# Output products by Strassen's algorithm, with all later steps in a new list

## The chip, the cores and the metric

The kernel runs on one core of one Trainium2 chip. The metric is the device time of one execution in microseconds. The core's engines are TensorE (PE in the profile; its weight loads are PEld), VectorE (DVE), ScalarE (ACT), GpSimd (POOL) and SyncE (SP), which here only issues DMAs. TensorE writes only into PSUM, which the kernel uses as four buffers of two banks (128 x 1024 fp32 each). GpSimd does no work out of PSUM in this kernel.

## The reference

```python
def _attn_ref(q, k, v, sort_net):          # batch 4, heads 8, seq 768, head_dim 64, 8 blocks of 96
    P = sort_net                           # (4, 8, 8, 8), five rounds of exp and row/column norms
    ...
    k_sorted = np.einsum('bhij,bhjcd->bhicd', P, k_b)
    v_sorted = np.einsum('bhij,bhjcd->bhicd', P, v_b)
    scores = scale * np.matmul(q_b, k_sb.transpose(0, 1, 2, 4, 3))     # inside a block
    attn = softmax(scores)
    return np.matmul(attn, v_sb)

def _moe_ref(x, w1, w2, w_out):            # x (3072, 512), w1, w2 (512, 1024), w_out (1024, 512)
    g = np.maximum(x @ w1, x @ w2)
    return g @ w_out                       # float32 (3072, 512)
```

## The kernel before

There are four batch items of 768 tokens. For each item the kernel mixes the blocks of k and of v with the Sinkhorn matrix (`sort_k`, `sort_v_pair` and its relatives, matrix products whose results go from PSUM to `kT` and `v_sb`), computes the scores of 8 units (`scores`: 8 small products, then one exponential on ScalarE into one of 8 buffers `e`), multiplies with the values (`values`: 8 products, then a reciprocal and a multiplication on VectorE), and transposes the result to `xT` (`x_transposes`: on TensorE for item 0, by a DMA from the SP queue for the others). The queries of items 2 and 3 are copied into pairs (`pair_q`) and transposed by two DMAs on SP (`q_transposes`). `turn_v` reorders the loaded v on chip, in four pieces for each pair of rows.

The second half uses max(a, b) = relu(a - b) + b. `w_difference` turns w1 into w1 - w2, `moe_h` computes the relu part into tiles `g` (8 tiles an item, each 128 x 2 x 384: two rows of 128 hidden features for half of the tokens, `ch`), and `w_product` computes `wc` = w2 @ w_out once. An item's output is then g @ w_out + x @ wc: a product of 768 tokens by 1536 features by 512 columns. In `out_products` it is done in six tiles of 128 tokens, each of 12 matmuls with a moving operand of 128x512 that accumulate in one bank; `moe_out` evicts two tiles at a time (128x1024) and stores 512 KB, and `moe_out_last` does the last two tiles in smaller pieces.

The order is written out by hand. Up to the step `h11b` of `front` all is item 0's attention, its `g` tiles and the transposed w2. From there a loop over the items runs through units (`moe_h`, `w_product`, `moe_out`), and the lists `first_tail`, `second_tail` and `third_tail` say which attention steps of the next item come after which unit. Each engine works through its instructions in that order; the steps differ in which engine evicts PSUM (`pick` and `evac` choose by running loads). The loads go through GpSimd's DMA queue, the stores and the DMA transposes through SP's.

Of the kernel before, what the change touches and what calls it, by code (L numbers as in the profile page):

```python
# [16 lines left out]
def kernel(  # L17
# [35 lines left out]
    NE = 8  # L53
# [188 lines left out]
    def turn_v(rows, eng, c0, c1):  # L242
        dst, src = v_dc[rows, 0 : D * BLK], v_raw[rows]
        if eng == "A":
            nc.scalar.copy(
                out=dst.rearrange("p (d c two) -> p d c two", c=BLK, two=2)[:, :, c0:c1],
                in_=src.rearrange("p (c d two) -> p d c two", c=BLK, two=2)[:, :, c0:c1],
            )
        else:
            nc.vector.tensor_copy(  # L250
                out=dst.bitcast(U32).rearrange("p (d c) -> p d c", c=BLK)[:, :, c0:c1],
                in_=src.bitcast(U32).rearrange("p (c d) -> p d c", c=BLK)[:, :, c0:c1],
            )
# [149 lines left out]
    def pair_q(b, two):  # L403

        if two == 0:
            q_pair[b] = qpool.tile([128, HP, R, 2 * D], BF16, tag="q_pair", name="q_pair", bufs=1)
        nc.vector.tensor_copy(
            out=q_pair[b][:, :, :, two * D : (two + 1) * D],
            in_=q_raw[b][:, two * HP : (two + 1) * HP].rearrange("p h (r d) -> p h r d", r=R),
        )  # L410
        load["D"] += 900
# [125 lines left out]
    e_tiles, x_tiles = {}, {}  # L537

    def scores(b, u, n=0):
# [15 lines left out]
        e = e_bufs[(b * 8 + u) % NE]  # L555
# [98 lines left out]
    def w_product(dmt):  # L654
# [9 lines left out]
        evac(wc[:, dmt, :], ps[:, 0:512], 512)  # L664
# [33 lines left out]
    out_ps = {}  # L698

    def out_products(dst, b, ti, n0=0, n1=512, part=None):  # L700
        ch, off = divmod(ti * 128, TCH)
        for m in range(NFB + HP) if part is None else range(part * 6, part * 6 + 6):
            hp = m - NFB
            nc.tensor.matmul(  # L704
                dst,
                g_tiles[b, ch, m // 2][:, m % 2, off : off + 128]
                if m < NFB
                else xT[:, b % 2, ch, hp % 2, hp // 2, off : off + 128],
                wo_sb[:, m, n0:n1] if m < NFB else wc[:, hp, n0:n1],
                start=(m == 0),  # L710
                stop=(m == NFB + HP - 1),
            )

    def moe_out(b, ti, part):
        slot = ti % 2
        if slot == 0 and part == 0:
            out_ps[0] = ps_f32("out_ps")
        ps = out_ps[0]
        out_products(ps[:, slot * 512 : (slot + 1) * 512], b, ti, part=part)
        if slot == 1 and part == 1:  # L720
            tok0 = b * S + ti * 128
            o = opool.tile([128, 2, 512], FP32, tag="o", name="o")
            evac(o.rearrange("p t n -> p (t n)"), ps, 1024)
            nc.sync.dma_start(
                out=out[tok0 - 128 : tok0 + 128, :].rearrange("(t p) n -> p t n", p=128),
                in_=o,
            )

    def moe_out_last(ti, pieces):

        tok0 = (B - 1) * S + ti * 128
        for n0, n1, eng in pieces:
            ps = ps_f32("out_ps")
            out_products(ps[:, 0 : n1 - n0], B - 1, ti, n0, n1)
            o = opool.tile([128, n1 - n0], FP32, tag=f"o{ti}{n0}", name="o", bufs=1)
            if eng == "A":
                nc.scalar.copy(out=o, in_=ps[:, 0 : n1 - n0])
            else:
                nc.vector.tensor_copy(out=o, in_=ps[:, 0 : n1 - n0])  # L739
# [107 lines left out]
    def turn(rows, c0):  # L847
        turn_v(rows, "D", c0, c0 + 24)
        load["D"] += 850

    def sorts_and_scores(b):
        SC, VA, TR = att(b)
        return SC, VA, TR, [lambda t=t: sort_k(b, t) for t in range(3)]

    SC, VA, TR, KS = sorts_and_scores(1)
    VS = [lambda t=t: sort_v_pair(2, t) for t in range(8)]
    TQ = [lambda half=half: q_transposes(1, half) for half in range(2)]
    TURN = [lambda c=c: turn(both, c) for c in (0, 24, 48, 72)]
    first_tail = {
        7: KS,  # L860
        9: [TQ[0], TURN[0]],
        10: [SC[0], TQ[1], TURN[1]],
        11: SC[1:4] + TURN[2:4] + [lambda half=half: load_v(3, half=half) for half in range(2)],
        12: VS[0:3],
        13: VS[3:6],
        14: VS[6:8] + [SC[4]],
        15: [VA[0], lambda: pair_q(2, 0)],
        16: [VA[1], lambda: pair_q(2, 1)],
        17: SC[5:8] + [TR[0]],
        18: [VA[2]],  # L870
        19: [VA[3], TR[1]],
        20: [VA[4]],
        21: [VA[5], TR[2]],
        22: [VA[6], VA[7], TR[3]],
    }
    SC, VA, TR, KS = sorts_and_scores(2)
    VS = [lambda t=t: sort_v_halved(3, t) for t in range(4)]
    TURN = [lambda c=c: turn(both, c) for c in (0, 24, 48, 72)]
    second_tail = {
        0: [lambda: q_transposes(2, 0), lambda: q_transposes(2, 1)],  # L880
        2: KS,
        4: SC[0:2],
        5: [VA[0]],
        6: SC[2:4] + [TURN[0]],
        7: [VA[1], TR[0]],
        8: [VA[2], TURN[1]],
        9: [VA[3], TR[1], TURN[2]],
        10: SC[4:7],
        11: [VA[4], TURN[3]],
        12: [VA[5], TR[2], lambda: load_k(3), lambda: load_q(3)],  # L890
        13: [VA[6]],
        14: SC[7:8] + VS[0:2],
        15: [VA[7], TR[3]],
        16: VS[2:4],
        17: [lambda: pair_q(3, 0)],
        18: [lambda: pair_q(3, 1)],
    }
# [70 lines left out]
```

## Time and profile before

| | before |
|---|---|
| device time, median of 3 runs | 165.8 us (165.71 to 165.83) |
| span of the profiled execution, first to last instruction | 165.0 us |
| TensorE busy | 157.0 us (95%) |
| VectorE busy | 77.5 us (47%) |
| ScalarE busy | 82.3 us (50%) |
| GpSimd busy | 33.9 us (21%) |
| mean granted TensorE clock | 0.999 |

The profiled execution has no separate device time beside its span. Its span is 0.8 us below the median of the runs, so 0.8 us lies around the span, and a time for the changed kernel is made as a span plus 0.8 us. In the timeline a matmul's duration runs to its modelled end and overlaps the next one's; a pace is therefore read as the distance between the starts of two groups, divided by the number of matmuls between them. The list that the change replaces begins at 38.40 us, where the first `sort_k` of item 1 follows the last `moe_h` of item 0, and TensorE's last matmul ends at 161.9 us.

### The profile page before, as it was taken

To read this page: it belongs to the slowest core of one execution; us is meant where nothing else is said; L and a number is where in the kernel's file an instruction comes from. 1 tells how busy PE (TensorE), PEld (TensorE's weight loads), DVE (VectorE), ACT (ScalarE), POOL (GpSimd) and SP (SyncE) were. 2 spreads that over 40 slices of the span, in tenths; PEclk is the share of its full clock that TensorE was granted. 3 is DMA by queue.
4 is the path that set the end of the run, shared out by engine and by line. 5 is a ranking of instruction groups with operands and counts; after the bars stand their busy time and mean duration, and the time that the engine had idled before them with its cause. 6 is when DMAs were issued, how large, how long until landed. Compare 5 with 4: busy or idle time off the path is not lost.

```text
span 165.0 us, 4561 instructions
## 1 busy us (share of the span) xinstructions
PE 157.0 (95%) x2007; PEld 95.4 (58%) x2025; DVE 77.5 (47%) x170; ACT 82.3 (50%) x101; POOL 33.9 (21%) x61
## 2 busy tenths in 40 slices
PE   7889999999999999999999999999999999999992
PEld 7839776756554555557655554575655546654451
DVE  4878995684366564525277763250642420000011
ACT  3489776617239846055652353457447206642020
POOL 7949997131206000000014010000000000000000
PEclk9999999999999999999999999999999999999999
DMA  3999999999999999689515999995025294000333
GB/s 41 204 204 194 164 196 207 209 205 220 210 203 204 220 224 167 175 84 228 111 19 104 126 212 157 200 309 29 0 52 175 50 164 142 0 0 0 127 131 127
DMA packets 30404, 23.90 MB, mean 145 GB/s; under 512 B 16752, under 2 KB 25200, under 8 KB 30384
## 3 DMA queue, kind: packets, MB, share of 16 engines
q0 software_dynamic: 11040, 13.37, 50.0%
q1 hardware_dynamic: 19200, 10.17, 28.9%
q8 instruction: 16, 0.26, 0.7%
q10 hardware_dynamic: 144, 0.07, 0.1%
q14 instruction: 4, 0.03, 0.1%
HBM read 26.75 MB, written 6.29 MB: 200 GB/s over the span
## 4 chain that ended last, share of the span: by engine, by line
PE 81%; DMA 6%; DVE 5%; ACT 3%; POOL 2%; issue 2%
PE out_ps L704 37%; PE h_ps L677 25%; DMA w_sb<-in_moe_w_dram 5%; PE wc_ps L657 4%; PE o_ps L575 4%; PE k_ps L458 3%; PE s_ps L548 3%; ACT e L556 1%; POOL w_sb L189 1%; PE v_ps L523 1%; DMA p_sb<-in_sort_net_dram 1%; PE tq_ps L433 1%; DVE colsum L276 1%; DVE p_sb L273 1%; PE tw_ps L638 1%
## 5 line engine op out<-in xcount | busy, mean ns | idle before, releaser
L704 PE MATMUL out_ps<-wo_sb,g 128*128 128x512 bf16 (+2 forms) x187 | 46.0, 370 | 1.4 <-issue 1.0
L677 PE MATMUL h_ps<-xT,w_sb 128*128 128x384 bf16 x256 | 44.5, 326 | 0.0
L677 PEld LDWEIGHTS <-w_sb 128*128 128x128 bf16 x256 | 24.0, 98 | 15.5
L556 ACT ACTIVATE e<-s_ps 96x768 bf16<-96x768 f32 x32 | 24.0, 805 | 14.8 <-PE s_ps L548 14.8
L691 ACT ACTIVATE g<-h_ps 128x768 bf16<-128x768 f32 x27 | 21.7, 811 | 17.4 <-PE h_ps L677 17.3
L704 PEld LDWEIGHTS <-g 128*128 128x128 bf16 x200 | 17.1, 97 | 15.8
L704 PE MATMUL out_ps<-wc,xT 128*128 128x512 bf16 (+2 forms) x98 | 24.7, 370 | 0.1
L108 ACT COPY o<-out_ps 128x1024 f32<-128x1024 f32 x10 | 10.1, 1012 | 28.0 <-PE out_ps L704 25.2
L592 DVE TENSOR_TENSOR x<-o_ps,rs 96x512 bf16<-96x512 f32 x32 | 22.0, 687 | 1.1
L704 PEld LDWEIGHTS <-xT 128*128 128x128 bf16 x100 | 9.6, 97 | 11.2
L575 PEld LDWEIGHTS <-e 96*128 96x128 bf16 x256 | 11.7, 97 | 5.7 <-DVE v_sb L110 0.2
L586 DVE RECIPROCAL rs<-o_ps 96x8 f32<-96x8 f32 x32 | 6.4, 201 | 17.2 <-PE o_ps L575 17.1
L739 DVE COPY o<-out_ps 128x512 f32<-128x512 f32 (+1 forms) x2 | 1.2, 625 | 27.6 <-PE out_ps L704 27.6
L575 PE MATMUL o_ps<-v_sb,e 96*128 96x65 bf16 x256 | 12.7, 193 | 0.0
L110 DVE CAST kT<-k_ps 128x1024 bf16<-128x1024 f32 x6 | 7.2, 1222 | 8.4 <-PE k_ps L458 8.4
L110 DVE CAST v_sb<-v_ps 96x1024 bf16<-96x1024 f32 x7 | 8.5, 1219 | 4.9 <-PE v_ps L523 2.2
L160 POOL DMA_DIRECT2D v_raw<-in_k_dram x3 | 2.5, 838 | 35.1 <-DVE v_dc L250 31.4
L108 ACT CAST v_sb<-v_ps 96x1024 bf16<-96x1024 f32 x9 | 8.8, 1015 | 1.6 <-PE v_ps L500 0.8
L169 POOL DMA_DIRECT2D v_raw<-in_v_dram x11 | 6.5, 593 | 12.7 <-DVE v_dc L250 6.4
L693 DVE TENSOR_SCALAR g<-h_ps 128x768 bf16<-128x768 f32 x5 | 4.8, 957 | 8.9 <-PE h_ps L677 8.8
L548 PEld LDWEIGHTS <-kT 64*128 64x128 bf16 x256 | 6.1, 94 | 4.8 <-issue 2.6
L548 PE MATMUL s_ps<-qT,kT 64*128 64x96 bf16 x256 | 8.5, 204 | 0.3 <-DVE qT L110 0.2
(97 smaller groups left out, 144.4 us busy)
## 6 DMA issues: line engine op xcount, KB each, us to landing
out_dram<-o SPq DMA_DIRECT2D x11, 512.0 KB, 3.4
v_raw<-in_v_dram POOLq DMA_DIRECT2D x8, 384.0 KB, 13.5
k_raw<-in_k_dram POOLq DMA_DIRECT2D x9, 256.0 KB, 11.0
w_sb<-in_moe_w_dram POOLq DMA_DIRECT2D x4, 256.0 KB, 6.0
w_sb<-in_moe_w_dram POOLq DMA_DIRECT2D x2, 512.0 KB, 9.6
wo_sb<-in_moe_w_out_dram POOLq DMA_DIRECT2D x2, 512.0 KB, 13.7
v_raw<-in_v_dram POOLq DMA_DIRECT2D x3, 256.0 KB, 5.0
q_raw<-in_q_dram POOLq DMA_DIRECT2D x4, 192.0 KB, 9.1
```

Source lines behind the costliest of these rows:

```text
L108: nc.scalar.copy(out=out_ap, in_=in_ap)
L110: nc.vector.tensor_copy(out=out_ap, in_=in_ap)
L169: nc.gpsimd.dma_start(out=v_raw[r0 : r0 + 64, m * n : (m + 1) * n], in_=v_src[b, :, m * n : (m + 1) * n],)
L548: nc.tensor.matmul(ps[:, h2 * 512 + ii * 128 : h2 * 512 + ii * 128 + BLK], kT[b][rows, (hp * 8 + i) * BLK : (hp * 8 + i) * BLK + 128], rhs ...
L556: nc.scalar.activation(out=e[:, 0 : 8 * BLK].rearrange("p (t c r) -> p t c r", t=8, r=R), in_=ps[0:BLK] .rearrange("p (t f) -> p t f", t=8 ...
L575: nc.tensor.matmul(ps[:, h2 * 512 + ii * 65 : h2 * 512 + (ii + 1) * 65], e[:, (h2 * 4 + ii) * BLK : (h2 * 4 + ii) * BLK + 128], v_sb[:, m0 ...
L586: nc.vector.reciprocal(out=rs, in_=ov[:, :, :, 64])
L592: nc.vector.tensor_tensor(out=x, in0=ov[:, :, :, 0:D], in1=rs.to_broadcast([BLK, 2, 4, D]), op=ALU.mult,)
L657: nc.tensor.matmul(ps[:, 0:512], w2T[:, fb, dmt * 128 : (dmt + 1) * 128], wo_sb[:, fb, :], start=(fb == 0), stop=(fb == NFB - 1),)
L677: nc.tensor.matmul(h_ps[ch, t][:, m * 512 : m * 512 + TCH], w1_sb[:, hp, fb * 128 : (fb + 1) * 128], xT[:, b % 2, ch, hp % 2, hp // 2, :], ...
L691: nc.scalar.activation(out=g, in_=src, func=AF.Relu)
L704: nc.tensor.matmul(dst, g_tiles[b, ch, m // 2][:, m % 2, off : off + 128] if m < NFB else xT[:, b % 2, ch, hp % 2, hp // 2, off : off + 12 ...
```

## The change

The output product of an item is computed by Strassen's algorithm in Winograd's form. Tokens are halved (`ch`), features are halved (four rows of g and two of x each), output columns are halved (`NW` = 256). Seven products of 384 tokens by 768 features by 256 columns take the place of eight. The sums that they need are formed on chip in bf16: four of g (two halves of 128x768 each) and four of x (128x768) for each item, four of w_out (128x1024) and four of wc (128x512) once. The late ones lie in the room of `w2T`, which `w_product` reads.

A `Group` runs the seven steps for two tiles of 128 tokens of each half (P) or for one (U). It holds one PSUM buffer from its first step to its last; the steps alternate between its two banks, and a step that accumulates on a bank comes after the eviction of that bank two steps before. A step is 12 (P) or 6 (U) matmuls with a moving operand of 128x256, then one eviction of 128x512 or 128x256. On VectorE (D) an eviction with an addition is one instruction; on ScalarE (A) it is a copy, and GpSimd does the addition in SBUF. Each group stores twice.

All steps from 38.40 us on stand in one list of tokens, run from left to right. A token is a kind, its numbers and the engine of its eviction or sum (A, D, or P for GpSimd): k, b sort k and v; s, v are scores and values; q, x transposes; t turns v; p copies queries; lv, lk, lq load item 3's v, k and q; w sums of weights (w0 of w_out, w1 of wc); c `w_product`; X, G sums of x and g; h `moe_h`; P, U steps of the output groups. Two pieces of `turn_v` and some of the sums go to GpSimd, three of the four `pair_q` copies to ScalarE; there are 6 buffers `e` instead of 8, taken in the order of the list; `q_pair` takes the room of `q_raw`. The steps up to 38.40 us stay. The removed lists and functions (`out_products`, `moe_out`, `moe_out_last`, the three tails and the loop over the items) are left out below.

```diff
     TCH = S // 2
     NFB = DFF // 128
-    NE = 8
+    NE = 6
+    NW = DMODEL // 2
...
-    def pair_q(b, two):
+    def pair_q(b, two, eng):
         if two == 0:
-            q_pair[b] = qpool.tile([128, HP, R, 2 * D], BF16, tag="q_pair", name="q_pair", bufs=1)
-        nc.vector.tensor_copy(
-            out=q_pair[b][:, :, :, two * D : (two + 1) * D],
-            in_=q_raw[b][:, two * HP : (two + 1) * HP].rearrange("p h (r d) -> p h r d", r=R),
-        )
-        load["D"] += 900
+            q_pair[b] = qpool.tile([128, HP, R, 2 * D], BF16, tag="q_raw", name="q_pair", bufs=1)
+        out = q_pair[b][:, :, :, two * D : (two + 1) * D]
+        in_ = q_raw[b][:, two * HP : (two + 1) * HP].rearrange("p h (r d) -> p h r d", r=R)
+        if eng == "A":
+            nc.scalar.copy(out=out, in_=in_)
...
-        e = e_bufs[(b * 8 + u) % NE]
+        e = e_bufs[e_next[0] % NE]
+        e_next[0] += 1
...
+    sums_g = big.tile([128, 3, 4, TCH], BF16, tag="sums_g", name="sums_g")
+    sums_x = big.tile([128, 4, 2, TCH], BF16, tag="sums_x", name="sums_x")
+    wt_early = big.tile([128, 2, 4, NW], BF16, tag="wt_early", name="wt_early")
+    w2T_flat = w2T.rearrange("p f d -> p (f d)")
+    wt_late = w2T_flat[:, 0 : 8 * NW].rearrange("p (n k f) -> p n k f", n=2, k=4)
+    wt_c = w2T_flat[:, 8 * NW : 16 * NW].rearrange("p (n k f) -> p n k f", n=4, k=2)
+    def weight_blocks(c):
+        t, k = (wc, 2) if c else (wo_sb, 4)
+        return [
+            t[:, i * k : (i + 1) * k, j * NW : (j + 1) * NW] for i in range(2) for j in range(2)
+        ]
+    def weight_sums(c, which, eng):
+        b11, b12, b21, b22 = weight_blocks(c)
+        t1, t3 = (wt_c[:, 0], wt_c[:, 2]) if c else (wt_early[:, 0], wt_early[:, 1])
+        t2, t4 = (wt_c[:, 1], wt_c[:, 3]) if c else (wt_late[:, 0], wt_late[:, 1])
+        out, in0, in1 = {
+            1: (t1, b12, b11),
+            2: (t2, b22, t1),
+            3: (t3, b22, b12),
+            4: (t4, b21, t2),
+        }[which]
+        eng.tensor_tensor(out=out, in0=in0, in1=in1, op=ALU.subtract)
+    def x_sums(b, which, eng):
+        a11, a12, a21, a22 = [xT[:, b % 2, ch, :, half, :] for ch in range(2) for half in range(2)]
+        s1, s2, s3, s4 = [sums_x[:, n] for n in range(4)]
+        out, in0, in1, op = {
+            1: (s1, a21, a22, ALU.add),
+            2: (s2, s1, a11, ALU.subtract),
+            3: (s3, a11, a21, ALU.subtract),
+            4: (s4, a12, s2, ALU.subtract),
+        }[which]
+        eng.tensor_tensor(out=out, in0=in0, in1=in1, op=op)
+    def g_sums(b, t, which, eng):
+        def a(ch, half):
+            return g_tiles[b, ch - 1, t + 2 * half - 2]
+        s1, s2, s4 = [sums_g[:, n, t * 2 : t * 2 + 2] for n in range(3)]
+        if which == 1:
+            out, in0, in1, op = s1, a(2, 1), a(2, 2), ALU.add
+        elif which == 2:
+            out, in0, in1, op = s2, s1, a(1, 1), ALU.subtract
+        elif which == 3:
+            out, in0, in1, op = a(2, 1), a(1, 1), a(2, 1), ALU.subtract
+        else:
+            out, in0, in1, op = s4, a(1, 2), s2, ALU.subtract
+        eng.tensor_tensor(out=out, in0=in0, in1=in1, op=op)
+    def left(b, which, k, off):
+        c = slice(off, off + 128)
+        if k < 4:
+            t, m = divmod(k, 2)
+            if which in (1, 2, 4):
+                return sums_g[:, {1: 0, 2: 1, 4: 2}[which], k, c]
+            ch, t = {"a11": (0, t), "a12": (0, t + 2), "a22": (1, t + 2), 3: (1, t)}[which]
+            return g_tiles[b, ch, t][:, m, c]
+        j = k - 4
+        if which in (1, 2, 3, 4):
+            return sums_x[:, which - 1, j, c]
+        ch, half = {"a11": (0, 0), "a12": (0, 1), "a22": (1, 1)}[which]
+        return xT[:, b % 2, ch, j, half, c]
+    def right(which, k):
+        if which in (1, 2, 3, 4):
+            if k >= 4:
+                return wt_c[:, which - 1, k - 4]
+            return (wt_early if which in (1, 3) else wt_late)[:, (which - 1) // 2, k]
+        half, n = {"b11": (0, 0), "b21": (1, 0), "b22": (1, 1)}[which]
+        n = slice(n * NW, (n + 1) * NW)
+        return wo_sb[:, half * 4 + k, n] if k < 4 else wc[:, half * 2 + k - 4, n]
+    class Group:
...
+        def product(self, bank, lw, rw, new):
+            n = 0
+            last = len(self.ks) * len(self.tiles) - 1
+            for k in self.ks:
+                for p, ti in enumerate(self.tiles):
+                    ins = nc.tensor.matmul(
+                        self.ps[:, bank * 512 + p * NW : bank * 512 + (p + 1) * NW],
+                        left(self.b, lw, k, ti * 128),
+                        right(rw, k),
+                        start=new and n == 0,
+                        stop=n == last,
+                        skip_group_check=True,
+                    )
+                    self.apart(ins, bank)
+                    n += 1
...
+        def add(self, ch, half, n, other, needs, eng, spare=False):
+            if eng == "A":
+                to = self.by_tile(self.a) if spare else self.part(ch, half)
+                ins = self.read(nc.scalar.copy(out=to, in_=self.by_tile(self.bank(n))), n, needs)
+                nc.gpsimd.tensor_tensor(out=self.part(ch, half), in0=to, in1=other, op=ALU.add)
+                return ins
+            ins = nc.vector.tensor_tensor(
+                out=self.part(ch, half), in0=self.by_tile(self.bank(n)), in1=other, op=ALU.add
+            )
+            return self.read(ins, n, needs)
+        def copy(self, out, n, eng):
+            if eng == "D":
+                ins = nc.vector.tensor_copy(out=out, in_=self.by_tile(self.bank(n)))
+            else:
+                ins = nc.scalar.copy(out=out, in_=self.by_tile(self.bank(n)))
+            return self.read(ins, n)
+        def store(self, ch):
+            tok0 = self.b * S + ch * TCH + self.tiles[0] * 128
             nc.sync.dma_start(
...
+                out=out[tok0 : tok0 + len(self.tiles) * 128, :].rearrange(
+                    "(t p) n -> p t n", p=128
+                ),
+                in_=self.o[ch],
+            )
+        def step(self, at, eng):
+            a = self.by_tile(self.a) if at else None
+            if at == 0:
+                n = len(self.tiles)
+                self.ps = ps_f32("out_ps")
+                self.a = opool.tile([128, self.w], FP32, tag=f"a{n}", name="a", bufs=1)
+                self.o = [
+                    opool.tile([128, n, DMODEL], FP32, tag=f"o{n}", name="o", bufs=2)
+                    for _ in range(2)
+                ]
+                self.product(0, "a11", "b11", True)
+                self.first = self.copy(self.by_tile(self.a), 0, eng)
+            elif at == 1:
+                self.product(1, 2, 2, True)
+                self.second = self.add(1, 0, 1, a, [self.first], eng)
+            elif at == 2:
+                self.product(0, "a12", "b21", False)
+                self.copy(self.part(0, 0), 0, eng)
+            elif at == 3:
+                self.product(1, 1, 1, False)
+                self.third = self.add(0, 1, 1, a, [self.first], eng)
+            elif at == 4:
+                self.product(0, 3, 3, True)
+                self.fourth = self.add(1, 1, 0, self.part(0, 1), [self.third], eng)
+            elif at == 5:
+                self.product(1, 4, "b22", False)
+                self.fifth = self.add(0, 1, 1, a, [self.first, self.fourth], eng)
+                self.store(0)
             else:
...
+                self.product(0, "a22", 4, False)
+                self.add(
+                    1, 0, 0, self.part(1, 0), [self.first, self.second, self.fifth], eng, True
+                )
+                self.store(1)
...
+        elif kind == "t":
+            turn_v(slice(0, 128), eng, n[1] * 24, n[1] * 24 + 24)
+        elif kind == "b":
+            (sort_v_pair if n[0] == 2 else sort_v_halved)(*n, eng)
+        elif kind == "p":
+            pair_q(*n, eng)
...
+        else:
+            key = kind, n[0]
+            if key not in groups:
+                groups[key] = Group(n[0], (0, 1) if kind == "P" else (2,), n[0] > 0)
+            groups[key].step(n[1], eng)
+    groups = {}
+    plan = [
+        """
+        X0.3D w0.3D c1A X0.1D G0.0.1D G0.1.1D k1.2D X0.2D k1.1A k1.0A q1.0D G0.1.2D q1.1A c0A
+        s1.2 s1.7 G0.0.2D t1.1D X0.4D s1.4 w0.1P c3D t1.0D c2A s1.3 P0.0A t1.3D s1.6 t1.2P w1.1D
+        s1.0 k2.0D lv0 w0.2D b2.4A w1.2D b2.0D k2.1A G0.1.4D b2.3A P0.1D w0.4D G0.1.3P b2.2A
+        b2.1A lv1 w1.3D P0.2A G0.0.3P b2.6A b2.7A b2.5D P0.3D k2.2A v1.2 v1.4 p2.0A P0.4A v1.7
+        U0.0A v1.3 p2.1A U0.1D G0.0.4D U0.2D s1.5 t3.0D q2.0 s1.1 U0.3A q2.1 U0.4A w1.4D v1.6
+        v1.5 x1.3 x1.2 P0.5D v1.1 P0.6D U0.5A s2.5 x1.1 s2.1 t3.1P v1.0 x1.0 U0.6D t3.2D s2.0
+        s2.3 s2.7 t3.3D v2.1 h1.1.2D h1.1.3D h1.1.1A b3.2D s2.2 h1.1.0D lq3 G1.0.1D X1.1D v2.3
+        h1.0.1A G1.1.1D h1.0.0A X1.2D G1.1.2D h1.0.3A lk3 v2.0 v2.7 h1.0.2A v2.5 G1.0.2D P1.0D
+        X1.3P p3.0A p3.1D s2.4 q3.0 s2.6 b3.1D P1.1D k3.1A q3.1 x2.0 G1.1.3D k3.0A k3.2D X1.4P
+        P1.2D v2.4 U1.0A v2.6 P1.3D b3.0A x2.3 v2.2 U1.1D U1.2A G1.0.3D x2.2 s3.1 s3.4 G1.1.4D
+        U1.3A G1.0.4D P1.4A x2.1 U1.4A P1.5A b3.3A s3.7 U1.5D P1.6A U1.6A s3.5 s3.0 s3.6 h2.1.1D
+        v3.1 h2.1.2A v3.5 h2.1.3D v3.4 X2.1P h2.1.0A v3.7 h2.0.1A X2.2P X2.4P G2.1.1D h2.0.0A
+        G2.0.1P s3.3 s3.2 G2.1.2D h2.0.2A v3.0 h2.0.3A U2.0D G2.0.2P x3.2 v3.3 G2.1.4D v3.6
+        G2.1.3D U2.1D U2.2A P2.0A G2.0.3P X2.3D x3.0 v3.2 P2.1D G2.0.4D x3.3 P2.2A U2.3A U2.4A
+        P2.3D x3.1 P2.4D P2.5D U2.5A U2.6D P2.6D h3.0.1A X3.1P h3.1.2A X3.3D h3.0.3A h3.1.3D
+        h3.1.1A X3.2D h3.1.0D G3.0.1D G3.1.1D X3.4D G3.1.3D h3.0.0A h3.0.2A G3.1.2D G3.1.4P
+        U3.0A G3.0.2D P3.0A G3.0.4P G3.0.3D P3.1A U3.1A P3.2D U3.2D U3.3D P3.3D P3.4D U3.4D
+        P3.5D P3.6D U3.5D U3.6D
+        """,
+    ]
+    for part in plan:
+        for text in part.split():
+            token(text)
```

## The prediction

> **What bounds the kernel now.** The page comes first: its busy times and its chain.
>
> ```profile
> PE 157.0 (95%) x2007; PEld 95.4 (58%) x2025; DVE 77.5 (47%) x170; ACT 82.3 (50%) x101; POOL 33.9 (21%) x61
> ...
> PE 81%; DMA 6%; DVE 5%; ACT 3%; POOL 2%; issue 2%
> ```
>
> TensorE is the bound. Then the windows from the new list's first step on, cut where the outputs of items 0 and 1 end.
>
> ```profile
> 38.40:71.10 32.70, 31.88 (x498) 18.16 (x506) 18.34 (x29) 17.07 (x22) 3.55 (x5) 1.00 1.03 202
> 71.10:104.10 33.00, 32.38 (x421) 18.75 (x423) 17.74 (x28) 15.61 (x19) 3.40 (x4) 1.00 0.88 132
> 104.10:162.00 57.90, 57.49 (x503) 31.91 (x507) 12.55 (x23) 25.10 (x31) 0.00 (x0) 1.00 0.43 99
> ```
>
> The columns are length, then PE, PEld, DVE, ACT and POOL busy. VectorE and ScalarE are about half idle in the first two windows, and VectorE is nearly free in the third. The pace of a matmul comes from starts in TensorE's timeline.
>
> ```profile
> 135.78 10.56 PE L677 MATMUL h_ps<-xT,w_sb 128*128 128x384 bf16 x64
> 146.18 1.89 PE L704 MATMUL out_ps<-wo_sb,g 128*128 128x512 bf16 x7
> ...
> 148.77 1.89 PE L704 MATMUL out_ps<-wo_sb,g 128*128 128x512 bf16 x8
> ...
> 161.08 0.61 PE L704 MATMUL out_ps<-wo_sb,g 128*128 128x128 bf16 x8
> 161.53 0.39 PE L704 MATMUL out_ps<-wc,xT 128*128 128x128 bf16 x4
> ```
>
> 384 columns: 10.40/64 = 162.5 ns. 512: 2.59/12 = 215.8 ns (an output tile has 12; one record is missing). 128: 0.45/8 = 56.3 ns, each with its own weight load, so loads hide at least down to that pace.
>
> **What it removes on TensorE.** Before, outputs are 276 x 215.8 + 12 x 162.5 + 12 x 56.3 ns = 62.2 us. After, 4 items x 7 products x 3 tiles x 6 = 504 matmuls of 256 columns. No row has that width; halfway between 128 and 384 it is (56.3 + 162.5)/2 = 109.4 ns, 55.1 us. Bounds: half of a 512 (107.9) and a 384 row (162.5, loads in the way); I take 109.4, since the line through three widths is straight. That saves 7.1 us, 1.77 an item, at most.
>
> The Trainium skill, "TensorE: Matmul & The Clock Gate", section "Back-to-back issue gap", speaks against this: it gives a sustained 81 ns for 128 columns and 131 for 512. By it 256 columns would take some 98 ns, and the outputs would go from 38 to 49 us, slower by 11. The 56.3 and 215.8 ns here contradict both figures, and the measurement decides.
>
> **What it adds.** Prices come from these rows.
>
> ```profile
> L592 DVE TENSOR_TENSOR x<-o_ps,rs 96x512 bf16<-96x512 f32 x32 | 22.0, 687 | 1.1
> L231 POOL TENSOR_TENSOR w_sb<-w_sb 128x1024 bf16<-128x1024 bf16 x2 | 4.3, 2146 | 0.4 <-DMA w_sb<-in_moe_w_dram 0.4
> L108 ACT CAST wc<-wc_ps 128x512 bf16<-128x512 f32 x3 | 1.8, 586 | 5.8 <-PE wc_ps L657 5.8
> L231 DVE TENSOR_TENSOR w_sb<-w_sb 128x1024 bf16<-128x1024 bf16 x2 | 1.3, 688 | 0.3 <-DMA w_sb<-in_moe_w_dram 0.3
> L739 DVE COPY o<-out_ps 128x512 f32<-128x512 f32 x1 | 0.7, 692 | 26.3 <-PE out_ps L704 26.3
> L739 DVE COPY o<-out_ps 128x384 f32<-128x384 f32 x1 | 0.6, 558 | 1.3 <-PE out_ps L704 1.3
> ```
>
> VectorE: 35 sums of 768 at 0.55 us (between 0.52, three quarters of 688 ns, and 0.69 itself), 19.3; 3 sums of w_out at 0.69 and 4 of wc at 0.42, 3.7; 18 P evictions at 0.69 and 13 U at 0.42 (the two L739 rows differ by 134 ns for 128 columns), 17.9. That is 41 us more, less 2.5 of old output evictions and 3.3 of two turns and three query copies that leave. ScalarE: 10 P at 0.59, 15 U at 0.37, three query copies at 1.5 (its 64x1536 copy took 1,516 ns), 16 us, less 10.4. GpSimd: 13 sums at 1.61 (three quarters of 2,146 ns), one of w_out at 2.15, 15 additions behind ScalarE's copies at 1.07 or 0.54, two turns (0.8 as on VectorE to 2.15; I take 1.6), about 37 us.
>
> Summing the list row by row from 38.40 us: TensorE 113.7 us, VectorE 84.8, ScalarE 66.5, GpSimd 44. In the first ten rows of the list it is 55.3, 54.3, 43.5 and 20.6: there VectorE has as much work as TensorE. From there on TensorE has 58.4 and VectorE 30.5. So the saving is safe in the second half and in question in the first, where the order also works against it: a P group and a U group hold two of four PSUM buffers, and TensorE can run only two evictions ahead.
>
> **Walking the list.** I followed it with those durations, each engine in order, a buffer free when its eviction ends. A stall is TensorE idle.
>
> (1) `q1.0` stands behind one `w_product` and the k sorts, so TensorE is there at 38.40 + 1.73 + 1.64 = 41.77. Item 1's q lands at 42.9: `load_q(2)` on GpSimd waited for it until 42.92. Before, two products of `w_product` (3.5 us) covered this. Stall 1.15 us (0 to 1.2).
>
> (2) From 46 to 66 us, second to fifth row: TensorE has about 20 us, VectorE and ScalarE about 19 each, all in order, with `b` and `k` evictions of 1.0 to 1.2 us through two or three free buffers. The walk gives 1.7 us of stalls (0 to 4: VectorE and ScalarE never behind, or behind by a fifth of their work). Behind a late eviction queue the `b` steps, then every `v`, as `values` needs all of `v_sb`. Before, this stretch had its own, from 49.15 to 51.85, where three exponentials came at once.
>
> (3) SP. Its transposes are slow to issue:
>
> ```profile
> 66.21 6.40 SPq L605 DMA_TRANSPOSE xT<-x  x3
> ...
> 74.17 4.52 SPq L419 DMA_TRANSPOSE qT<-q_pair  x2
> ```
>
> In the walk `p2.1A` ends at 66.4; q2.0 and q2.1 take SP to 70.9 and x1.3 to 72.7 (1.2 to 6.40/3 = 2.1 us); x1.2 lands 3.8 us after its issue there (the DMA rows' median), at 76.5. `h1.1.2`, which needs it, is up at 74.4. Stall 2.1 us (0 to 4; before, q2 came after the x transposes). Stores and x1.1, x1.0 queue behind on SP, but `h1.0.1` comes 6 us later.
>
> (4) Item 1's outputs, VectorE close behind TensorE: 0.65 us more (0 to 2).
>
> The walk reaches `U0.6` at 73.0; before, the same work (71.11, plus 2.04 for k2 and two `s` that it did later) ends at 73.15. It reaches `U1.6` at 106.35; before, 104.14 + 2.23 for k3 and three `s` = 106.37. Stalls of 5.6 us against 2.15 eat the first two items' 3.5 us. From `U1.6` on 51.4 us remain, and the walk finds each sum ready before its step (the GpSimd chain X2.1 to G2.0.2 is done 2 us early, x3.1 has 5.2 us before `h3.0.1`); before, 0.7 us of stalls lay there, and I take 0.3. TensorE ends at 106.35 + 51.4 + 0.3 = 158.05.
>
> The end: after the last matmul before come 0.27 (eviction), 1.7 (64 KB landing) and 1.1 us more. After, 0.42, 2.0 (the 256 KB store of before) and 1.1, 3.5 us; at most 1.0 more, since the last four stores move 1.5 MB and the best microsecond of before moved 387 GB/s. Span 161.55, time with the 0.8 around it 162.35; I say 162.3.
>
> Costed at nothing: the six `e` buffers (in list order every buffer's `v` stands before its next `s`), `q_pair` in `q_raw`'s room (its transposes are long done), 16 stores for 12 (SP, under matmuls), and item 3's loads on GpSimd's queue. There `lq3` and `lk3` stand behind `t3.1P` and some additions, and are issued near 76 us, 10 us before use. `lv0` and `lv1` go out near 53 and 57 us, the second behind one sum; `t3.0D` is up at 67. A 384 KB piece of v took 13.5 us to land among others and a 256 KB piece 5.0, so 10 us may just do; if not, `t3.0D` waits up to 3 us, and every VectorE eviction behind it.
>
> **Rivals.** *TensorE bound throughout* (0.25): the stalls stay as before and the whole 7.1 comes, 165.0 - 7.1 + 0.45 + 0.8 = 159.2. For it: each stall above is small beside estimates in a walk of 68 us. Against: 54.3 against 55.3 us in ten rows.
>
> *VectorE held up by GpSimd* (0.18), slower: rows two to five hold GpSimd work of 2.15 + 1.6 + 2 x 1.61 + 1.07 = 8 us beside VectorE's own sums, which have no slack there. If these exclude each other, half of it on VectorE's path gives +4.0, 166.3, all of it 170.3. It decides once 3.5 us are lost. For it: no row of before has the two engines summing in SBUF together, so nothing excludes it. Against: the steps lie at different places in the list.
>
> The Trainium skill, "SBUF — State Buffer", section "SBUF: two separate sides", says that a VectorE operation with two SBUF inputs and a GpSimd operation that reads SBUF take a shared port pair as an exclusive lock. By it a sum that meets the 2.15 us w_out sum would wait for all of it; no row of before shows such a pair.
>
> *Nothing left* (0.05): 1 us or so more in (2) or (3) twice over, and a late t3.0, 165.5 to 166.1. *The narrow matmul does not hold its pace* (0.02): at 120 ns, 5.3 us more, 167.6; the 56.3 ns row is against it.
>
> **How the numbers follow.** The forecast has 0.50. Faster by over 0.2% (0.3 us, about what a measurement can tell): 0.50 + 0.25 and 0.02 of the edge case, 0.77; within 0.2%, the other 0.03 of it; slower, 0.18 + 0.02 = 0.20. Of the fast rival 0.06 and of the slower one 0.09 lie outside the range. The range runs from 158.8 (full gain, a little fewer stalls) to 167.0 (the lower part of the slower rival); the forecast's own is 160.5 to 165.
>
> **What would show it.** In the changed profile: 256-column groups 109 ns apart in starts; TensorE busy down by about 7 us; gaps of TensorE near 42 us (q landing), 50 to 65 and 74 to 77 us (xT); `h2` beginning near 107 and `h3` near 133 us; no gaps after. It is wrong if the pace is above 115 ns, if VectorE's sums take over 0.8 us where GpSimd is busy, or if item 2's stage has gaps.

## The result, and the profile after

The changed kernel takes 180.1 us (179.7 to 180.6) against 165.8 us: ratio 1.085 (95% interval 1.082 to 1.089), 14.3 us slower where 3.5 us faster was forecast, and outside the range. The span of its profiled execution is 178.8 us against 165.0, 13.8 us more. Medians below are over all runs of a kernel; ratios leave out runs over 1.5% slower than the fastest of the same kernel, and the profiled executions of e2 and e7 are such runs. From the page:

```profile
PE 157.0 (88%) x2226; PEld 118.5 (66%) x2229; DVE 116.9 (65%) x233; ACT 87.4 (49%) x118; POOL 73.8 (41%) x92
...
PE   7999989998993999979207999999999999999980
...
PEclk9999999999999699999955799999999999999999
...
PE 69%; DMA 15%; DVE 8%; issue 2%; POOL 2%; ACT 1%; DVEq 0%
```

A slice is 4.47 us. TensorE has two holes, in the slice with the 3 (53.6 to 58.1 us) and in those with 2 and 0 (84.9 to 93.9), and the clock row drops in the slice behind the first and from the second half of the other on. DMA's share of the chain went from 6% to 15%. TensorE's busy time is the same 157.0 us although there is less for it to do, in part because matmuls at a lower clock count as busy. The windows, cut where the outputs of items 0 and 1 end, with the columns length, PE, PEld, DVE, ACT and POOL busy, clock, DMA share (1 is full) and GB/s:

```profile
38.00:77.65 39.65, 35.45 (x676) 26.67 (x678) 32.74 (x49) 26.23 (x35) 14.56 (x14) 0.96 0.85 157
77.65:122.05 44.40, 34.59 (x486) 25.20 (x482) 24.50 (x43) 19.00 (x27) 11.20 (x11) 0.88 0.68 119
122.05:173.60 51.55, 51.55 (x486) 39.85 (x484) 30.14 (x52) 18.15 (x29) 21.12 (x16) 1.00 0.27 82
```

TensorE is idle for 4.2 us in the first stage and 9.8 us in the second, and never in the third. TensorE's timeline (start, length, line, count, and in brackets the idle time ahead with what ended it) names the holes:

```profile
58.05 1.03 PE L808 MATMUL out_ps<-w2T,sums_g 128*128 128x256 bf16 x8 [2.67 <-DVE w2T L726]
...
79.74 4.07 PE L680 MATMUL h_ps<-xT,w_sb 128*128 128x384 bf16 x24 [0.81 <-DMA xT<-x]
...
94.77 6.77 PE L680 MATMUL h_ps<-xT,w_sb 128*128 128x384 bf16 x24 [8.79 <-DMA xT<-x]
...
144.64 1.04 PE L808 MATMUL out_ps<-wt_early,g 128*128 128x256 bf16 x8
145.51 0.60 PE L808 MATMUL out_ps<-wc,sums_x 128*128 128x256 bf16 x4
...
173.16 0.60 PE L808 MATMUL out_ps<-w2T,g 128*128 128x256 bf16 x4
```

The pace is there: 0.87 us for eight matmuls of 256 columns, 109 ns each. The long hole is `h1.0.1` at 94.77, which waits 8.79 us for x1.0 and x1.1 by DMA. The 24 matmuls behind it take 6.77 us; the same 24 at 79.74 take 4.07. The other hole is `P0.1` at 58.05, which waits 2.67 us for the sum w0.2.

**The long hole.** SyncE's timeline, and then GpSimd's:

```profile
80.07 4.32 SPq L608 DMA_TRANSPOSE xT<-x  x2
```

```profile
53.12 1.66 POOL L754 TENSOR_TENSOR g<-g 128x768 bf16<-128x768 bf16 x1
54.71 1.06 POOL L170 DMA_DIRECT2D v_raw<-in_v_dram  x2
55.79 1.65 POOL L754 TENSOR_TENSOR g<-g 128x768 bf16<-128x768 bf16 x1
...
80.57 0.93 POOL L144 DMA_DIRECT2D v_raw<-in_q_dram  x1 [1.72 <-DVE rs L589]
81.50 1.61 POOL L161 DMA_DIRECT2D v_raw<-in_k_dram  x3
```

x1.1 and x1.0 go out from 80.07 us on. In the same four microseconds GpSimd issues `lq3` (768 KB) and the three pieces of `lk3` (768 KB together). The list has `lk3` behind `h1.0.3A`, whose matmuls are the last eight of the group at 94.77 us, but GpSimd has nothing of its own to do ahead of it. It issues the loads as soon as the last turn of v has freed `v_raw`, 13 us before that group begins. In the chain of waits, in order of time:

```profile
82.32 12.41 DMA xT<-x
```

The transpose, about 4 us elsewhere, lands after 12.41. Windows of the hole, and behind it:

```profile
86.00:88.00 2.00, 0.00 (x0) 0.00 (x0) 1.93 (x5) 0.00 (x0) 0.00 (x0) 1.00 1.30 196
92.00:94.00 2.00, 0.00 (x0) 0.00 (x0) 0.00 (x0) 0.00 (x0) 0.00 (x0) 0.50 1.00 241
96.00:98.00 2.00, 2.00 (x8) 0.96 (x7) 0.00 (x0) 0.45 (x1) 2.00 (x2) 0.50 0.00 0
```

Until 94 the DMA engines are full at about 200 GB/s and nearly all of the core waits. From 90 us on the clock is 0.50, and it stays there for 5.5 us after the work has come back (the window from 100 to 102 us has 0.93), which costs 6.77 - 4.07 = 2.7 us more.

**The short hole.** VectorE's timeline, the first sum of w_out beside GpSimd and a later one of the same size without:

```profile
54.21 3.79 DVE L726 TENSOR_TENSOR w2T<-wo_sb,wt_early 128x1024 bf16<-128x1024 bf16 x1
...
60.46 0.68 DVE L726 TENSOR_TENSOR w2T<-wo_sb,w2T 128x1024 bf16<-128x1024 bf16 x1
```

The sum begins while GpSimd adds in SBUF (G0.1.3P, from 53.12) and ends after GpSimd's next sum (G0.0.3P, 55.79 to 57.44) has ended. Windows behind the hole:

```profile
59.00:60.00 1.00, 1.00 (x23) 0.70 (x23) 1.00 (x3) 0.00 (x0) 0.00 (x0) 0.66 1.14 234
...
61.00:62.00 1.00, 1.00 (x7) 0.69 (x6) 0.47 (x2) 1.00 (x2) 0.00 (x0) 0.50 0.72 152
62.00:63.00 1.00, 1.00 (x8) 0.58 (x7) 0.00 (x0) 0.10 (x1) 0.00 (x0) 0.63 0.10 18
```

With 0.50 from 60 to 61 as well, these four microseconds hold 2.3 at full clock, so the slow clock costs about 1.7 more.

**The end.** The last matmul ends at 173.8 (173.16 + 0.60), 5.0 us ahead of the span's end; before, it was 3.1. Windows:

```profile
173.00:174.00 1.00, 0.76 (x7) 0.43 (x5) 0.71 (x3) 0.00 (x0) 0.00 (x0) 1.00 1.03 377
...
175.00:176.00 1.00, 0.00 (x0) 0.00 (x0) 0.00 (x0) 0.00 (x0) 0.00 (x0) 1.00 1.03 387
176.00:177.00 1.00, 0.00 (x0) 0.00 (x0) 0.00 (x0) 0.00 (x0) 0.00 (x0) 1.00 0.96 359
```

The last four stores (1.5 MB) keep the DMA engines full for four microseconds.

**The sum.** Narrower outputs -7.05; the long hole with its clock 8.79 + 2.70 = +11.5; the short one 2.67 + 1.7 = +4.4; the end +2.0. That is +10.8 of the 13.8. TensorE's other idle time (0.77 before q1.0's transposes end, 0.81 for x1.2, and smaller ones) is 4.2 + 9.8 - 8.79 - 2.67 = 2.5 us against 1.85 from the list's start before; with the list's start 0.3 us earlier that adds 0.4. Some 2.6 us are not placed; the section behind the experiments comes back to them.

### The profile page after: what moved, and what is told of

The parts are those of the page before. It is cut to its first block, busy times and chain, and to the rows that moved or that the text cites. A ratio compares the mean times of both kernels' runs of the same rounds, so it can differ in the third digit from the quotient of the medians.

```text
span 178.8 us, 5142 instructions
## 1 busy us (share of the span) xinstructions
PE 157.0 (88%) x2226; PEld 118.5 (66%) x2229; DVE 116.9 (65%) x233; ACT 87.4 (49%) x118; POOL 73.8 (41%) x92
## 4 chain that ended last, share of the span: by engine, by line
PE 69%; DMA 15%; DVE 8%; issue 2%; POOL 2%; ACT 1%; DVEq 0%
PE out_ps L808 30%; PE h_ps L680 23%; DMA xT<-x 9%; DMA w_sb<-in_moe_w_dram 5%; PE wc_ps L660 4%; PE o_ps L578 3%; PE k_ps L460 3%; DVE w2T L726 2%; PE s_ps L550 2%; POOL w_sb L190 1%; DVE x L595 1%; PE v_ps L525 1%; PE tq_ps L435 1%; DMA p_sb<-in_sort_net_dram 1%; DVE colsum L277 1%
## 5 line engine op out<-in xcount | busy, mean ns | idle before, releaser
L832 POOL TENSOR_TENSOR o<-o,a 128x256 f32<-128x256 f32 (+1 forms) x8 | 6.8, 860 | 34.0 <-ACT o L831 34.0
L808 PEld LDWEIGHTS <-sums_g 128*128 128x128 bf16 x144 | 13.8, 98 | 4.4 <-issue 2.7
L834 DVE TENSOR_TENSOR o<-out_ps,a 128x512 f32<-128x512 f32 (+1 forms) x16 | 9.4, 586 | 10.0 <-PE out_ps L808 5.5
L696 DVE TENSOR_SCALAR g<-h_ps 128x768 bf16<-128x768 f32 x9 | 8.6, 957 | 9.9 <-PE h_ps L680 9.7
L808 PE MATMUL out_ps<-wo_sb,g 128*128 128x256 bf16 x96 | 14.0, 285 | 0.0
L808 PE MATMUL out_ps<-w2T,sums_x 128*128 128x256 bf16 x72 | 11.9, 274 | 0.0
L831 ACT COPY o<-out_ps 128x256 f32<-128x256 f32 (+1 forms) x13 | 5.6, 439 | 10.4 <-PE out_ps L808 10.2
L738 POOL TENSOR_TENSOR sums_x<-xT 128x768 bf16<-128x768 bf16 x3 | 5.2, 1735 | 11.8 <-issue 11.8
L808 PEld LDWEIGHTS <-sums_x 128*128 128x128 bf16 x96 | 8.9, 98 | 1.2
L832 POOL TENSOR_TENSOR o<-o 128x256 f32<-128x256 f32 (+1 forms) x5 | 4.7, 943 | 11.9 <-ACT o L831 11.7
```

Of the source, the lines that this page charges most:

```text
L696: nc.vector.tensor_scalar(out=g, in0=src, scalar1=0.0, scalar2=None, op0=ALU.max)
L808: ins = nc.tensor.matmul(self.ps[:, bank * 512 + p * NW : bank * 512 + (p + 1) * NW], left(self.b, lw, k, ti * 128), right(rw, k), start=n ...
L832: nc.gpsimd.tensor_tensor(out=self.part(ch, half), in0=to, in1=other, op=ALU.add)
L834: ins = nc.vector.tensor_tensor(out=self.part(ch, half), in0=self.by_tile(self.bank(n)), in1=other, op=ALU.add)
```

## The experiments

Two theories stood for the long hole. *Loads*: item 3's loads take the DMA engines from x1.1 and x1.0. *SyncE*: transposes and stores queue there, whatever else moves. For the short hole it is *exclusion* (VectorE waits while GpSimd sums) against *VectorE simply late*. The kernel before, run beside these, had medians of 166.2 to 166.6 us; where two kernels are compared, their ratios to it are.

**e1, the loads earlier.** k3 goes into k_raw's own room and q3 into another one, so that both can leave near 58 to 70 us, each held back by what its room last held.

```diff
-            if b < 3
+            if b < 4                       # load_k: k3 in k_raw's room
...
-            t = v_raw[:, HB * D :]...
+            t = kpool.tile([128, HB * D], BF16, tag="k_raw", name="q_raw3")...
...
-  P0.2A G0.0.3P b2.6A ... k2.2A v1.2 ... h1.1.0D lq3 G1.0.1D ... h1.0.3A lk3 v2.0
+  P0.2A G0.0.3P lk3 b2.6A ... k2.2A lq3 v1.2 ... h1.1.0D G1.0.1D ... h1.0.3A v2.0
```

> Item 3's loads of k and q go into the two k buffers that are free early (k at about 57 us, q after the last sort_k of item 2, about 66 us), when the DMA engines are idle from 63 to 72 us, and not into v's buffer at 80.6 to 83.1 us. Theory (loads): x1.1 and x1.0, issued on SP at 80.1 and about 82.3 us, landed only at 94.7 because 1.5 MB of loads were issued in the same three microseconds; TensorE's 8.8 us wait before h1.0.1 and the 2.7 us of half clock behind it go: 180.1 - 11.5 = 168.6 us, h1.0.1 near 86 us. Rival (SP): the transposes are late of themselves, behind SP's three stores and each other: h1.0.1 stays near 94 us, 179 to 181 us.

169.25 us, ratio 1.019 (1.012 to 1.026): 11 us of the 14 are back, by two loads in other places and nothing else. TensorE's and SyncE's timelines of e1:

```profile
75.42 0.52 PE L550 MATMUL s_ps<-qT,kT 64*128 64x96 bf16 x16 [1.89 <-DMA qT<-q_pair]
...
79.81 4.08 PE L680 MATMUL h_ps<-xT,w_sb 128*128 128x384 bf16 x24 [1.53 <-DMA xT<-x]
...
85.88 4.07 PE L680 MATMUL h_ps<-xT,w_sb 128*128 128x384 bf16 x24
```

```profile
67.90 6.60 SPq L421 DMA_TRANSPOSE qT<-q_pair  x2
```

`h1.0.1`, now at 85.88, has no wait and runs in 4.07 us. That speaks for the loads and against SyncE, whose steps are the same: it issues x1.1 and x1.0 from 80.08 us on, for 80.07 in the changed kernel. A smaller copy of the fault has moved ahead: q2's two transposes now lie beside the early q3 load and hold SyncE for 6.60 us (3.35 in the changed kernel), and TensorE waits 1.89 for them.

**e2, the two GpSimd sums to VectorE.**

```diff
-  ... w0.4D G0.1.3P b2.2A b2.1A lv1 w1.3D P0.2A G0.0.3P b2.6A ...
+  ... w0.4D b2.2A b2.1A lv1 w1.3D P0.2A G0.1.3D G0.0.3D b2.6A ...
```

> The two sums G0.1.3 and G0.0.3 move from GpSimd to VectorE, after P0.2; nothing else changes. Theory (exclusion): w0.2 on VectorE took 3.79 us and not 0.69 because GpSimd's two sums lay beside it; TensorE's wait of 2.67 us before P0.1 and about 1.6 us of half clock behind it go, VectorE gets 1.1 us of sums where it is idle: 180.1 - 4.3 = 175.8 us. Rival (evictions): TensorE would wait there for VectorE's and ScalarE's evictions anyway: within 1 us of 180.1.

177.4 us, ratio 1.062 (1.054 to 1.071), 0.023 below the changed kernel's, or 3.8 us, give or take 1.5. VectorE's timeline of e2:

```profile
55.87 0.68 DVE L726 TENSOR_TENSOR w2T<-wo_sb,wt_early 128x1024 bf16<-128x1024 bf16 x1
```

The sum takes 0.68 instead of 3.79 us although VectorE has two sums more to make, and the wait ahead of `P0.1` is gone. In e3 and e9, which have this edit too, it takes 0.68 as well; in e1, e4 and e5, which do not, 2.77 to 3.02. It is exclusion, not load. The long hole stays (8.9 us).

**e3, both together.** e1's edit and e2's.

> Both edits together. If the two losses are independent: 180.1 - 11.5 - 4.3 = 164.3 us, a little under the kernel before (165.8). If an earlier h1 stage or TensorE's earlier arrival meets the next late transfer (x1.2, v3 turns), part comes back: 166 to 170 us.

168.8 us, ratio 1.014 (1.008 to 1.020). If the two gains added, the ratio would be 1.019 - 0.023 = 0.996; 2.9 of e2's 3.8 us are lost again, give or take 2. TensorE's timeline of e3:

```profile
74.08 0.52 PE L550 MATMUL s_ps<-qT,kT 64*128 64x96 bf16 x16 [0.69 <-DMA qT<-q_pair]
...
78.49 5.71 PE L680 MATMUL h_ps<-xT,w_sb 128*128 128x384 bf16 x24 [1.55 <-DMA xT<-x]
```

Counted from the list's start (37.72 us in e1, 38.39 in e3), TensorE comes to `h1.1` 2.0 us sooner than in e1: the wait for w0.2, still 1.66 in e1, is gone, and that for q2 is 0.69 instead of 1.89. But the wait for x1.2 is the same, and the 24 matmuls behind it run at a lower clock (5.71 us instead of 4.08), which takes 1.6 of the 2.0 back. What follows: a stall taken away can come back as a slower clock behind the next one.

**e4, only k3 early.** The `load_k` half of e1, with `lk3` behind `G0.0.3P`; `lq3` as in the changed kernel.

> The changed kernel with only item 3's k loaded early (768 KB issued behind G0.0.3 near 57 us); q of item 3 stays where it was. Theory (bytes): the transposes x1.1 and x1.0 get through when the bytes issued beside them have passed; with half of the 1.5 MB gone they land some 4 us earlier, near 90 us, h1.0.1 with them, and the half-clock stretch shortens too: 173 to 176 us. Rival (any load in that queue holds them as long): 179 to 181 us; rival (k alone is to blame): 169 us.

176.9 us, ratio 1.053 (1.046 to 1.061). TensorE's timeline of e4:

```profile
91.07 6.21 PE L680 MATMUL h_ps<-xT,w_sb 128*128 128x384 bf16 x24 [6.16 <-DMA xT<-x]
```

With half of the bytes away 6.16 us of the wait are left of 8.79, over two thirds; `h1.0.1` begins 3.7 us sooner, about what 768 KB take at 200 GB/s (3.9). In time, by the ratios, 5.3 us come back of e1's 11.0, in part ahead of `P0.1`, where this execution waits 1.90 us and not 2.67; the median is a little above what was expected. So q3's load alone holds the transposes up as well, and the loss grows with the bytes, but it was not shown to be in proportion to them.

**e5, the clock alone.** 40 matmuls on zeros fill TensorE's wait ahead of `h1.0.1`.

```diff
-            moe_h(*n, eng=eng)
+            moe_h(*n, eng=eng, n=20480 if tuple(n) == (1, 0, 1) else 0)
```

> The changed kernel with 40 matmuls of 512 columns on zeros (8.6 us) put ahead of h1.0.1, which waits 8.8 us for its transpose; they write into the bank that h1.0.1 overwrites. Theory (idle halves the clock): the 24 matmuls of h1.0.1 to h1.0.3 take 3.9 us as elsewhere and not 6.6, and the rest is as it was: 180.1 - 2.7 = 177.4 us. Rival (the clock is low for another reason, as the loads' end): they stay at 6.6 us, 180 us.

179.1 us, ratio 1.076 (1.072 to 1.080). TensorE's timeline of e5:

```profile
84.08 8.80 PE L83 MATMUL h_ps<-fill 128*128 128x512 bf16 x39
94.12 4.06 PE L680 MATMUL h_ps<-xT,w_sb 128*128 128x384 bf16 x24 [1.24 <-DMA xT<-x]
```

The transposes land as late as before (94.12), but the 24 matmuls take 4.06 us instead of 6.77, so the idle time is what halves the clock. The last matmul ends at 170.4 instead of 173.8 us, 2.7 of it by the clock. In time only about 1.6 us appear (177.4 us was expected): in its profile the end behind the last matmul takes 6.7 us instead of 5.0. Why was not settled.

**e6, q3 late instead of early.** From e3: q3 goes back to `v_raw`'s room, its load behind a sum that GpSimd has to wait for.

```diff
-  ... k2.2A lq3 v1.2 ...   X1.3P p3.0A ...
+  ... k2.2A v1.2 ...       X1.3P lq3 p3.0A ...
```

> As the kernel with both edits (168.8 us), but item 3's q is loaded into v's buffer behind X1.3 on GpSimd, which waits for x1.0, so near 86 us and not at 63 us. Theory (loads again): in that kernel the early q load lay beside the transposes q2.0 to x1.2, which took SP 5.4 us for two and not 3.4, and TensorE waited 0.7 us for qT and 1.55 us for xT and then had 1.6 us of half clock; 3 to 4 us go, and q lands near 91 us, just before p3.0 wants it near 92: 165 to 166 us. Rival (the transposes are as slow without any load): 168 to 169 us. If q lands after p3.0 wants it, ScalarE blocks and the gain is lost again.

167.6 us, ratio 1.008 (1.004 to 1.011), above the 165 to 166 expected. The wait for q2 is gone, and that for x1.2 is 0.66 us at full clock. The bill comes later, in TensorE's timeline of e6:

```profile
93.69 1.90 PE L460 MATMUL k_ps<-bd,k_raw 64*64 64x64 bf16 x96 [1.31 <-ACT e L559]
```

ScalarE stands idle for 1.89 us at `p3.0A`, which waits for q3 until 91.46, and an exponential is queued behind it.

**e7 and e8, stores in halves.** e7 is e3 with each half of `o` in a tile of its own, so four stores for a group instead of two. e8 is e6 with that and with `c0A` moved ahead of `q1.0D`.

```diff
-                self.store(0)
+                self.store(0, 1)      # and (0, 0), (1, 1), (1, 0), each behind its last write
```

> As the kernel with both edits (168.8 us), but each group's outputs are stored in halves of 256 columns as soon as they are final (32 stores of half the size for 16). Theory (the end is bound by the stores): in the changed kernel the DMA engines move 375 to 387 GB/s without a gap from 173 to 177 us, so the 1.5 MB of the last four stores set the end 5.2 us after the last matmul; with half of that 0.75 MB, 1.5 to 2.0 us go: 166.8 to 167.3 us. Rival (the end is the latency of the last store): 168.8 us or more, since SP issues twice as many.

> All edits: both sums off GpSimd, k of item 3 early and q behind X1.3, stores in halves, and c0 ahead of q1.0 in the list, so that the q load of item 1 (42.9 us) is covered by two products as in the kernel before (about 1.2 us). If all is independent: 168.8 - 3.5 - 1.7 - 1.2 = 162.4 us, faster than the kernel before by 2%. If the stalls only move: 165 us or more, no gain.

168.8 us, ratio 1.012 (1.007 to 1.017), and 166.9 us, ratio 0.999 (0.996 to 1.003): both missed what was expected. In e7 the end behind the last matmul falls to 3.8 us, but SyncE waits for the early halves. SyncE's timeline of e7:

```profile
59.81 7.93 SPq L848 DMA_DIRECT2D out_dram<-o  x3
67.85 6.79 SPq L421 DMA_TRANSPOSE qT<-q_pair  x2
```

q2's transposes come behind three stores, 1.0 us after the copy that they need has ended (66.80), and also lie beside the q3 load; TensorE waits 3.12 us for qT. In e8 the stores hold SyncE in the same way (8.32 us from 59.63), and the move of `c0A` puts a 1.53 us wait on ScalarE's copy of q1. Here more stores cost time where SyncE has a transpose behind them.

**e9, all of it in its place.** e6; `c0A` ahead of `q1.0D` with `c3D` behind `q1.1A`; `s2.4` and `s2.6` ahead of `p3.0A`; half stores for item 3 alone, where no transposes follow.

```diff
-  k1.0A q1.0D G0.1.2D q1.1A c0A ... w0.1P c3D t1.0D ... lq3 p3.0A p3.1D s2.4 q3.0 s2.6
+  k1.0A c0A q1.0D G0.1.2D q1.1A c3D ... w0.1P t1.0D ... lq3 s2.4 s2.6 p3.0A p3.1D q3.0
...
+                if self.b == B - 1:
+                    self.store(0, 0)
```

> On top of the kernel with q behind X1.3 (167.6 us): only item 3's outputs are stored in halves, so the middle keeps its 12 whole stores; c0 stands ahead of q1.0 and c3 behind q1.1, so that both the q load and ScalarE's eviction of qT (1.43 us) are covered by a product; s2.4 and s2.6 stand ahead of the query copies, so that ScalarE does their exponentials while q lands. If the three stalls read from the traces (1.3 us of the end, 0.9 of q1, 1.3 before k3) are independent: 167.6 - 3.5 = 164.1 us, 1.3% under the kernel before. If stalls only move, 166 us or more.

163.2 us, ratio 0.981 (0.978 to 0.984): faster than both kernels. Its page:

```profile
PE 152.8 (95%) x2229; PEld 116.5 (73%) x2229; DVE 115.6 (72%) x235; ACT 87.5 (54%) x118; POOL 70.0 (44%) x90
...
PE   7999999999999999997999999999999999999991
...
PEclk9999999999999999999999999999999999999999
```

No holes and the full clock throughout; TensorE's longest wait in the list is 0.90 us.

**e10, e9 with whole stores.** Item 3's four half stores a group are two whole ones again.

> The same without the halved stores of item 3. Theory (the end is bound by the bytes of the last stores): the span ends 5.2 us after the last matmul and not 3.9, and the time is 1.3 us above the kernel beside it, 165.4 us. Rival (the last store's latency sets the end): both kernels within 0.4 us.

165.0 us, ratio 0.991 (0.988 to 0.994): 1.8 us slower than e9. Windows of e10 at its end:

```profile
158.00:159.00 1.00, 0.31 (x3) 0.03 (x1) 0.55 (x2) 0.00 (x0) 0.00 (x0) 1.00 1.03 371
...
160.00:161.00 1.00, 0.00 (x0) 0.00 (x0) 0.00 (x0) 0.00 (x0) 0.00 (x0) 1.00 1.05 387
```

The last matmul ends at 158.3 us of a span of 163.3, in e9 at 157.1 of 160.6: 5.0 us are left behind it and 3.5 in e9. In e10 the DMA engines are full at 371 to 387 GB/s for three microseconds of that. So bytes that are stored late set the end, by 1.5 us of the span.

## Why the prediction was wrong, point by point

**What held.** *The pace*: 109.4 ns were taken, 109 measured. *From `U1.6` on*: 51.7 us were walked, 51.55 measured, without a gap; so the saving of the second half is whole. *The unit prices*, in the groups kept apart by shape:

```profile
L738 DVE TENSOR_TENSOR sums_x<-xT 128x768 bf16<-128x768 bf16 x5 | 2.9, 574 | 0.0
L754 DVE TENSOR_TENSOR sums_g<-g,sums_g 128x768 bf16<-128x768 bf16 x6 | 3.2, 546 | 0.0
L738 POOL TENSOR_TENSOR sums_x<-xT,sums_x 128x768 bf16<-128x768 bf16 x2 | 3.3, 1630 | 0.1
L834 DVE TENSOR_TENSOR o<-out_ps,a 128x512 f32<-128x512 f32 x10 | 6.9, 688 | 5.3 <-PE out_ps L808 5.2
```

Where nothing collides they are 0.55 to 0.57, 1.63 and 0.69 us, for 0.55, 1.61 and 0.69. GpSimd's additions were 1.27 and 0.72 us for 1.07 and 0.54, with no wait of TensorE behind them. *The small stalls* came where they were put: 0.77 us at q1.0 (1.15 forecast) and 0.81 at x1.2 (2.1).

**The step that failed is (3), with what was costed at nothing.** It priced SyncE's queue and let each transpose land 3.8 us after its issue. It saw that x1.1 and x1.0 queue there and gave them 6 us of slack. Separately it put `lq3` and `lk3` "near 76 us, 10 us before use", at no cost. The two were never laid side by side: 1.5 MB of loads at about 200 GB/s are over 7 us of full DMA engines, in just the microseconds when the transposes needed them. The prediction had the transposes' issue, the loads' issue and the rate (202 GB/s in its first window), so that they collide could have been worked out. TensorE had x1.1 and x1.0 14.7 us after SyncE began to issue them (80.07 to 94.77); with the loads moved away, in e1, GpSimd's sum that waits for them begins after 5.5 (80.08 to 85.60), and 11 us come back.

**A term that no step had: the clock.** 2.7 us behind the long hole and about 1.7 behind the short one are matmuls at 0.50 of the clock. e5 shows the first by itself. In the profile of before the clock was 1.00 in every window shown, so no row gave the price, and the prediction put it at nothing without a reason. The Trainium skill, "TensorE: Matmul & The Clock Gate", Part 1, says that TensorE goes to half its clock after an idle window of about 3.4 us and comes back after about as long a busy one; the 8.79 us hole agrees with it, and the drop after the 2.67 us hole, and after one of 1.69 in e5, shows that less can do.

**The rival of VectorE held up by GpSimd** had 0.18 and its price was 4.0 to 8.0 us. It happened as it was put, in the rows named, at 4.4 by the trace and 3.8 by e2, the low end, and with the sign that the prediction names for being wrong (a sum of VectorE's over 0.8 us where GpSimd is busy). The argument against it, that the steps lie at different places in the list, was the same fault as in (3): the list orders steps within one engine, not across two. The Trainium skill, "SBUF — State Buffer", section "SBUF: two separate sides", which the prediction had weighed, is shown here: 3,787 ns beside GpSimd's sums and about 688 without. It states that the loser waits for the whole instruction; here it waited through the rest of one and all of the next, with two load issues between.

**The end** was put 0.45 us above that of before and came 2.0 above it: 5.0 us for 3.5, more than the bound of 1.0 on top (1.5 MB at 387 GB/s) allowed. The full DMA engines were the right row.

**The walk of the first two items** has a fault left even where nothing waits. In e9 the stretch from the list's start (37.53) to the end of item 1's outputs (105.4) takes 67.9 us with 2.2 us idle; before, the same work took 68.0 with 1.4 idle by its windows, where the walk had 2.15. And most of that 1.4 was not idle time. TensorE's timeline of before, and then of e9:

```profile
49.79 1.46 PE L704 MATMUL out_ps<-wo_sb,g 128*128 128x512 bf16 x6
51.18 1.13 PE L523 MATMUL v_ps<-bd,v_dc 64*128 64x64 bf16 x48
52.46 0.38 PE L704 MATMUL out_ps<-wo_sb,g 128*128 128x512 bf16 x1 [0.16 <-issue]
```

```profile
49.94 0.60 PE L808 MATMUL out_ps<-wc,xT 128*128 128x256 bf16 x4
50.48 0.51 PE L550 MATMUL s_ps<-qT,kT 64*128 64x96 bf16 x16
...
61.59 0.60 PE L808 MATMUL out_ps<-w2T,sums_x 128*128 128x256 bf16 x4
62.02 0.29 PE L578 MATMUL o_ps<-v_sb,e 96*128 96x65 bf16 x4
```

The tile of before shows seven of its eight products with w_out: the gap of 0.16 us stands where the record of the eighth is missing. Six such gaps make 1.0 us, so before had about 0.5 us idle and 67.5 of work, against 2.2 and 65.7 in e9. TensorE's work fell by 1.8 us there and not by the 3.5 forecast, and its waits grew by as much, while the second half saved all. Of the missing 1.7 a part is seen in the starts: four output matmuls of e9 take 0.54 us where products of s follow (49.94 to 50.48) and 0.43 where products of values follow (61.59 to 62.02). Before has 7 places where products for k, s or v follow output matmuls, e9 has 13, and 0.1 us each is 0.6 us. About 1 us stays open. The 2.6 us that the sum above does not place are of these three kinds: 1.0, 0.6 and about 1.

In figures: the forecast of 162.3, plus 11.5 for the long hole, 4.4 for the short one and 1.5 for the end is 179.7; measured, 180.1. That this comes so near is luck in part: the walk's own stalls of 5.6 us, where 2.5 came besides the holes, and work that did not fall as far as it forecast about cancel in it.

## What to carry to other kernels

The order of a list holds only within one engine: here a load left as soon as its buffer was free, 13 us ahead of the matmuls that its row stands behind, so lay every transfer's earliest start beside the DMA transposes that TensorE waits for, and hold a load back by a data dependency or move it ahead. Price a stall of TensorE with the slower clock behind it, and two engines that sum in SBUF as one where they can meet. Gains measured one at a time need not add (e3); and what is stored after the last matmul can end the kernel at the DMA engines' rate. A small gap in a trace can be a missing record: count the instructions before calling it idle.

## What the runs showed of the hardware that was not expected

- A DMA transpose that lands in about 4 us elsewhere took 12.41 us beside 1.5 MB of loads; its issue is held up too, 3.30 us for one of q2's pair in e1 beside a load and 1.68 without.
- The granted clock fell to 0.50 about 4 us after the start of the 8.79 us hole and again just behind the 2.67 us one. The length of a wait does not decide it alone: waits of 1.89 and 1.66 us in e1 left the clock full, one of 1.69 in e5 did not. What decides was not tried. Once it fell it stayed at 0.50 for about 3.4 us or two or three times that: 59.3 to 62.7 and 90.0 to 100.3 us in the changed kernel, 88.6 to 95.5 in e4.
- A VectorE sum with both inputs in SBUF went from 0.69 to 3.79 us beside two GpSimd sums that had two DMA issues between them. In e1, e4 and e5, where the same pair meets a little differently, it took 2.77 to 3.02.
- Stores alone moved 359 to 387 GB/s, where loads and transposes together moved about 200.
